# A fused layer's forward and backward pass: feed-forward spread over the table chain, gates by chunk, turned weights in the weights' slots, state sums begun beside the last d h

## The chip, the cores and the metric

The kernel runs on one core of one Trainium2 chip. The core has a matrix engine (TensorE, PE in the profile, with PEld for its weight loads), a vector engine (VectorE, DVE), a scalar engine for functions and copies (ScalarE, ACT), GpSimd (POOL), a queue engine that only issues transfers (SyncE, SP), and 16 DMA engines. Each engine works through a queue of its own in order; the engines meet by semaphores. The metric is the time of one execution on the device in microseconds; lower is better.

## The reference

A state-space convolution, gated by a feed-forward net, with a residual, forward and backward (L = 2048 rows, D = 512, N = 128 states, F = 1792):

```python
xn = _layernorm(x)
dt = exp(log_dt);  K[d,l] = Re sum_n C[d,n] exp(dt*A[d,n]*l) dt*B[d,n]     # A, B, C complex
y  = irfft(rfft(pad(xn)) * rfft(pad(K)))[:L] + xn * Dskip                  # s: the long convolution
o  = silu(xn @ w1) @ w2;   g = silu(o)                                     # the feed-forward gate
out = x + s * g
# and, by jax.vjp with grad_out, the gradients of x, A_re, A_im, B_re, B_im, C_re, C_im, log_dt, Dskip, w1, w2
```

With G for grad_out the backward pass needs ds = G * silu(o) (into the convolution's backward) and do = G * s * silu'(o) (into the feed-forward's backward); then d h = (do @ w2^T) * silu'(h), d x = d h @ w1^T, dW2 = silu(h)^T do, dW1 = xn^T d h, and the gradients of the state parameters from dK.

## The kernel before

The 2048 rows lie as 128 partitions by 16 tiles (t), the 512 channels as 4 blocks b of 128. The code is made of Python generators; each `yield` ends a step, and the helpers `interleave`, `woven`, `paced`, `until` and `after` decide how the steps of several generators are mixed. The text's order gives each instruction its rank. When the program is built, each engine's queue is laid out from these ranks and from what is ready, so an instruction can stand ahead of one that comes earlier in the text; on the chip each queue then runs in the order that was laid out.

- Setup (L1032 to L1052): loads x, weights and parameters, layer norm to `xn`, constants, DFT matrices `TF`, `TI`, `F2`, `I2`.
- `chain()` (L1065): for each block, `gen_tables` (17 steps) builds exponential tables `E` and `Y` on VectorE and ScalarE (the sines `sn`, L420), and the convolution kernel by matmuls (`ps_k` L452, `ps_e` L463), copied to `KE` and stored in `Kd`; `gen_conv_x` (4 steps) transforms `xn`; `gen_conv_fwd` of the block before (9 steps) loads the kernel as `Kb`, transforms it, multiplies the spectra (`cplx_mul`, L324), transforms back and adds the skip (`S_b`, L524), stored in `Sd`. The chain holds the forward convolutions of blocks 0 to 2.
- A forward transform (`dft_fwd`, L277) is 32 matmuls (`ps_s` L286) into `dA`, one transposing DMA `dB<-dA` (L289), three steps later 32 matmuls (L298, L299). The inverse (`dft_inv`, L304) is 32 matmuls (L311), copies, 32 matmuls (L320).
- `gen_ffn_fwd` (L532): 8 chunks of 256 rows, each 7 steps of `ps_h` (L546, copied to `hT`, stored in `Hd` by GpSimd's queue, silu to `aT`) and 2 of `ps_o` (L561, copied to `ob`, stored in `Od`). It runs as the outer loop, with 1.4 chain steps for each of its 72 (L1070).
- `gen_gate_rows` (L569): after the feed-forward, loads `Od` into `do` and grad_out into `G` (two buffers), and makes `ds` and the first factor of `do` on ScalarE, GpSimd and VectorE, mixed with what is left of the chain (L1077). `gate_s` (L595) and `gen_gate_s` multiply `do` by s, block by block.
- `gen_conv_fwd(k, 3)` (L1091) with the transposing loads of `W2T` (L1087) and the first backward transform beside it.
- `gen_conv_bwd` (L629), one block after the other: forward transform of `ds` (in `w8b` buffers, two), product with the spectrum of `xn` and inverse to `dK`, product with that of K and inverse to `du`. Beside it `gen_ffn_da` (L850): per chunk 7 steps of `ps_da` (L879) and 2 of `ps_dx` (L890), with `W1T` loaded in its first step (L860); and `gen_out` (L609), the output rows. Weights 1, 2, 1 (L1096).
- Last, with pools opened anew (L1099): `gen_ssm_bwd` (L808), the state sums: `ssm_fold` (loads `GE`, matmuls L685, L687, copy `Gf`), `ssm_v` (L718), `ssm_products` (`Tp`, L728), `ssm_sums` (`psS`, L740, L744), `gen_ssm_grads`; beside it `gen_dw2` (`ps_w` L922, a chunk of 128 columns of F per step), then `gen_dw1` (`ps_w` L940, 28 steps of 16 matmuls), and `gen_ln_bwd`.

SP issues nearly all loads and the transposes; ScalarE's queue the stores of `Kd` and `dKd`; GpSimd's queue the other stores (`k.st`). Memory is given by pools; a pool that opens where another closed must wait for the old tiles' last readers.

## Time and profile before

| | us |
|---|---|
| runs shown (3) | 764.97, 772.21, 774.16; median 772.21 |
| the profiled execution | 774.27, span 772.5 |
| mean granted TensorE clock | 0.907 |

Where the named work stands in the profiled execution (first and last start, from the rows of the tiles):

| work | from | to |
|---|---|---|
| feed-forward: ps_h, ps_o | 14.6 | 250.2 |
| tables' matmuls ps_k | 71.2 | 271.1 |
| gates: first silu (L583), last gate product (L591) | 264.2 | 304.8 |
| last forward convolution: Kb issued, last product of do with S_b | 290.1 | 333.7 |
| d h and d x: ps_da, ps_dx | 336.3 | 529.5 |
| backward convolutions' last inverse (L320) | | 507.3 |
| state sums psS | 561.6 | 724.1 |
| dW1's matmuls (L940) | 683.2 | 764.1 |

A busy time is the time in which the engine held an instruction; matmuls overlap, so that a full TensorE shows more matmul time than it gives columns. The idle time of an engine matters only where nothing else is the bound of that stage, so the profile is read by stages. DMA shares are the mean over 16 engines and can pass 1.

### The profile page before, as it was taken

The numbers are of one execution on the slowest core, as the hardware profiler recorded it, in microseconds if no ns is written. First come the engines' busy times: TensorE is split into PE (matmuls) and PEld (weight loads), VectorE is DVE, ScalarE is ACT, GpSimd is POOL, SyncE is SP. The second block draws the span as 40 slices with busy tenths as digits, with TensorE's granted clock in tenths as the row PEclk, the third lists the DMA queues.
The fourth block names the chain that finished last, engine by engine and source line by source line (L and its number), as shares of the span: only waits on it lengthen the run. The fifth ranks groups of instructions, "written<-read, shape, count | busy, mean of one in ns | idle before, by whom it ended". The sixth has DMA issues, their size and how long they took to land. (4 is left out here: it accounts for less than half of the span.)

```text
span 772.5 us, 13734 instructions
## 1 busy us (share of the span) xinstructions
PE 599.6 (78%) x5388; PEld 428.5 (55%) x5388; DVE 551.2 (71%) x1118; ACT 501.8 (65%) x700; POOL 87.3 (11%) x167
## 2 busy tenths in 40 slices
PE   3378878988979533578888798994489977899795
PEld 2244554754755333356566475672466654678675
DVE  6987997795775997489787696961163876998500
ACT  6877766877779575459878597750286677864121
POOL 2120100000000144000000000000000003130230
PEclk9699988999999785799999899997599998999998
DMA  9877866588667949999969768234899999776482
GB/s 270 305 165 240 233 212 167 231 232 239 240 189 206 348 159 212 292 307 321 269 199 259 193 183 223 65 116 108 209 221 223 270 302 255 194 140 129 79 172 71
DMA packets 218097, 163.18 MB, mean 211 GB/s; under 512 B 143024, under 2 KB 196272, under 8 KB 214192
## 3 DMA queue, kind: packets, MB, share of 16 engines
q1 hardware_dynamic: 205056, 139.75, 67.7%
q0 software_dynamic: 6224, 18.10, 6.8%
q10 hardware_dynamic: 6752, 4.46, 1.9%
q8 instruction: 42, 0.69, 0.4%
q14 instruction: 23, 0.19, 0.1%
HBM read 65.40 MB, written 62.26 MB: 165 GB/s over the span
## 5 line engine op out<-in xcount | busy, mean ns | idle before, releaser
L42 ACT CAST dA<-ps_s 128x1024 bf16<-128x1024 f32 x96 | 93.8, 1031 | 40.4 <-PE ps_s L299 24.6
L728 DVE TENSOR_TENSOR Tp<-Vb,Eb 128x1344 bf16<-128x1344 bf16 x64 | 52.6, 854 | 22.7 <-ACT Vb L42 13.7
L546 PE MATMUL ps_h<-XT,W 128*128 128x256 bf16 x448 | 61.0, 283 | 8.2 <-ACT hT L42 6.8
L42 ACT CAST dB<-ps_i 128x1024 bf16<-128x1024 f32 x48 | 46.9, 1018 | 27.5 <-PE ps_i L311 21.3
L561 PE MATMUL ps_o<-W,aT 128*128 128x512 bf16 x224 | 59.7, 408 | 5.1 <-ACT aT L554 3.9
L311 PE MATMUL ps_i<-I,sp_in 128*128 128x256 bf16 x384 | 53.0, 287 | 12.4 <-DVE sp_in L334 11.1
L298 PE MATMUL ps_s<-dB,F 128*128 128x512 bf16 x96 | 41.5, 432 | 25.6 <-DMA dB<-dA 23.1
L879 PE MATMUL ps_da<-doT,W2T 128*128 128x256 bf16 x448 | 56.5, 275 | 2.9 <-DVE dhT L881 2.9
L940 PE MATMUL ps_w<-dh_tok,xn 128*128 128x256 bf16 x448 | 53.0, 273 | 1.4 <-DMA dh_tok<-DHd 1.0
L546 PEld LDWEIGHTS <-W 128*128 128x128 bf16 x448 | 44.5, 102 | 17.2 <-issue 7.8
L890 PE MATMUL ps_dx<-W1T,dhT 128*128 128x512 bf16 x224 | 53.8, 380 | 0.0
L922 PE MATMUL ps_w<-do,a_tok 128*128 128x512 bf16 x224 | 53.0, 385 | 0.0
L311 PEld LDWEIGHTS <-sp_in 128*128 128x128 bf16 x384 | 37.5, 102 | 25.9 <-DVE sp_in L334 14.5
L286 PEld LDWEIGHTS <-TF 128*128 128x128 bf16 x384 | 27.4, 106 | 43.3 <-DMA Kb<-Kd 17.3
L879 PEld LDWEIGHTS <-W2T 128*128 128x128 bf16 x448 | 43.8, 99 | 12.4 <-issue 4.9
L42 ACT CAST Vb<-ps_v 128x672 bf16<-128x672 f32 x64 | 42.6, 723 | 9.4 <-PE ps_v L718 7.9
L42 ACT CAST o<-ps_w 128x256 bf16<-128x256 f32 (+1 forms) x42 | 18.6, 442 | 43.6 <-PE ps_w L940 31.7
L940 PEld LDWEIGHTS <-xn 128*128 128x128 bf16 x448 | 42.8, 98 | 7.1 <-issue 2.6
L881 DVE SCALAR_TENSOR_TENSOR dhT<-dhT,ps_da 128x512 bf16<-128x512 bf16 x56 | 37.2, 681 | 12.9 <-PE ps_da L879 12.6
L299 PE MATMUL ps_s<-dB,F 128*128 128x512 bf16 x96 | 41.4, 431 | 0.0
L561 PEld LDWEIGHTS <-aT 128*128 128x128 bf16 x224 | 22.0, 104 | 29.6 <-issue 7.4
L452 PEld LDWEIGHTS <-Y 128*128 128x128 bf16 x512 | 26.3, 106 | 21.7 <-DVE Y L439 11.2
(226 smaller groups left out, 1365.5 us busy)
## 6 DMA issues: line engine op xcount, KB each, us to landing
Yd<-Y SPq DMA_DIRECT2D x8, 1024.0 KB, 5.4
sp_in<-Ud SPq DMA_DIRECT2D x8, 1024.0 KB, 7.0
...
```

The costliest lines, as they stand in the source:

```text
L42: return self.nc.scalar.copy(out=out, in_=in_)
L298: nc.tensor.matmul(out=ps[:, 4 * u:4 * u + 4], lhsT=F2[:, m0], rhs=B[:, 0, g0:g0 + 4, :], start=True, stop=False)
L299: nc.tensor.matmul(out=ps[:, 4 * u:4 * u + 4], lhsT=F2[:, m1], rhs=B[:, 1, g0:g0 + 4, :], start=False, stop=True)
L311: nc.tensor.matmul(out=ps[:, g], lhsT=Y[:, c, g0 + g, :], rhs=k.I2[:, c].rearrange("p c m -> p (c m)"), start=(c == 0), stop=(c == 1))
L546: nc.tensor.matmul(out=ps[:, j], lhsT=k.W1[:, dk, ft * P:ft * P + P], rhs=XTv[:, :, dk, :], start=(dk == 0), stop=(dk == DK - 1))
L561: nc.tensor.matmul(out=ps[:], lhsT=aT[:, ft, t * P:t * P + P], rhs=k.W2[:, ft, :], start=(ft == 0), stop=(ft == FT - 1))
L728: k.nc.vector.tensor_tensor(out=Tp[:, c, :, r ^ c].rearrange("p e (q w) a -> p q w e a", w=2), in0=Vb[:, :, c].rearrange("p q w (e a) -> p ...
L879: nc.tensor.matmul(out=ps[:, j], lhsT=W2T[:, dk, ft * P:ft * P + P], rhs=dTv[:, :, dk, :], start=(dk == 0), stop=(dk == DK - 1))
L881: nc.vector.scalar_tensor_tensor(out=dh[:, i0:i0 + 2, :], in0=dh[:, i0:i0 + 2, :], scalar=1.0, in1=ps[:], op0=ALU.add, op1=ALU.mult)
L890: nc.tensor.matmul(out=ps[:], lhsT=dhs[ft // 8][:, ft % 8, t * P:t * P + P], rhs=k.W1T[:, ft, :], start=(ft == 0), stop=(ft == FT - 1))
L922: nc.tensor.matmul(out=ps[:], lhsT=at[:, t, :], rhs=k.do[:, t, :], start=(t == 0), stop=(t == k.T - 1))
L940: nc.tensor.matmul(out=ps[:], lhsT=k.xn[:, t, dk * P:dk * P + P], rhs=dh[:, t].rearrange("p j n -> p (j n)"), start=(t == 0), stop=(t == k ...
```

## The change

It does seven things.

1. The chain becomes the outer loop and the feed-forward is drawn at 0.45 steps for each chain step. What is left of the feed-forward runs beside the last forward convolution and the gates, with weights 3, 1, 1.
2. The gates go by chunk of two tiles, as the feed-forward gives them: `rows_done` says how far it is; the last chunks are read from `ob` in place instead of loaded from `Od`. grad_out is loaded at once (`Gr`). The product with s of blocks 0 to 2 is part of the gate, that of block 3 follows the convolution.
3. `do` takes the memory of the two `Y` tables, `ds` and the gates that of the table pool.
4. `W2T` is loaded into `W1`'s slot, in the last feed-forward chunk, and `W1T` into `W2`'s, by four transposes in the first d h steps.
5. `dft_fwd` runs its first half by component and turns each component by a DMA of its own.
6. `gen_conv_bwd` weaves the forward transform of the next block with the rest of this one, on six buffers; its spectra are loaded a step earlier, and so are the loads of `gen_out`. It is the outer loop (1.7 steps of d h and output rows for each).
7. The state sums begin when the backward convolutions are issued, half a step for each step of d h that is left; then they go on beside dW2 and dW1.

Smaller things: the last `Sd` store moves to ScalarE's queue, and `gen_ssm_grads` copies its turned rows back into `outb`.

```diff
+BR, SR = 1.7, 0.5
...
-def dft_fwd(k, w8, U, ev, tag="w8"):
+def dft_fwd(k, w8, U, ev):
-    A = w8.tile([P, 2, 16, P], BF16, name="dA", tag=tag)
+    A = w8.tile([P, 2, 16, P], BF16, name="dA", tag="w8")
     Av = A[:].rearrange("p c g (t e) -> p c g t e", e=8)
-    for h in range(2):
-        for c in range(2):
+    B = w8.tile([P, 2, 16, P], BF16, name="dB", tag="w8")
+    for c in range(2):
+        for h in range(2):
             ps = pc.tile([P, 8, P], F32, name="ps_s1", tag="pc")
             for j in range(8):
                 nc.tensor.matmul(out=ps[:, j], lhsT=k.TF[:, 8 * h + j, c, :], rhs=U(8 * h + j), start=True, stop=True)
             ev(Av[:, c, :, 8 * h:8 * h + 8, :], ps[:].rearrange("p t (g e) -> p g t e", e=8))
-    B = w8.tile([P, 2, 16, P], BF16, name="dB", tag=tag)
-    nc.sync.dma_start_transpose(B[:].rearrange("p c g k -> p (c g) k"), A[:].rearrange("p c g k -> p (c g k)"))
+        nc.sync.dma_start_transpose(B[:, c], A[:, c].rearrange("p g k -> p (g k)"))
     for _ in range(LAG):
         yield
...
-    nc.sync.dma_start(k.Sd[b], S[:].rearrange("p t d -> p (t d)"))
+    (nc.scalar if b == 3 else nc.sync).dma_start(k.Sd[b], S[:].rearrange("p t d -> p (t d)"))
...
-        ob = fp.tile([P, 2, D], BF16, name="ob", tag="ob", bufs=1)
+        if c == T // 2 - 1:
+            k.W2T = k.wt.tile([P, DK, k.F], BF16, name="W2T", tag="wa")
+        ob = fp.tile([P, 2, D], BF16, name="ob", tag="ob", bufs=2)
         for t in range(2):
             ps = k.pf.tile([P, D], F32, name="ps_o", tag="pf")
             for ft in range(FT):
                 nc.tensor.matmul(out=ps[:], lhsT=aT[:, ft, t * P:t * P + P], rhs=k.W2[:, ft, :],
                                  start=(ft == 0), stop=(ft == FT - 1))
             k.evf(ob[:, t], ps[:])
+            if c == T // 2 - 1:
+                for i in (2 * t, 2 * t + 1):
+                    nc.sync.dma_start_transpose(k.W2T[:, :, 448 * i:448 * i + 448], k.ins["B_w2"][448 * i:448 * i + 448, :])
             yield
         k.st(k.Od[:, 2 * c:2 * c + 2, :], ob[:])
-
-
-
-def gen_gate_rows(k, gp):
+        k.rows_done = c + 1
+        if k.late:
+            k.ob[c] = ob
+
...
+def gen_gate_rows(k, gp, lag):
 
     nc = k.nc
     TT = nc.vector.tensor_tensor
...
-    for t in range(0, 16, 8):
-        nc.sync.dma_start(k.do[:, t:t + 8, :], k.Od[:, t:t + 8, :])
-    for t0 in range(0, 16, 4):
-        G = gp.tile([P, 4, k.D], BF16, name="G", tag="G", bufs=2)
-        nc.sync.dma_start(G[:], k.g_v[:, t0:t0 + 4, :])
-        for t in range(t0, t0 + 4, 2):
-            ts = slice(t, t + 2)
-            Gt = G[:, t - t0:t - t0 + 2, :]
-            o = k.do[:, ts, :]
-            g = gp.tile([P, 2, k.D], BF16, name="g", tag="g", bufs=3)
...
-            TT(out=k.ds[:, ts, :], in0=Gt, in1=g[:], op=ALU.mult)
...
+    last = k.T // 2
+    Gr = gp.tile([P, k.T, k.D], BF16, name="Gr")
+    for t in range(0, k.T, 4):
+        nc.sync.dma_start(Gr[:, t:t + 4, :], k.g_v[:, t:t + 4, :])
+    for c in range(last):
+        while k.rows_done <= c or (c not in k.ob and k.rows_done < min(c + 1 + lag, last)):
             yield
-
-
-def gate_s(k, b, t0, n, S):
-
-    do = k.do[:, t0:t0 + n, b * P:b * P + P]
-    k.nc.vector.tensor_tensor(out=do, in0=do, in1=S, op=ALU.mult)
-
-
-def gen_gate_s(k, b, gp):
-    for t in (0, 8):
-        S = gp.tile([P, 8, P], BF16, name="S", tag="go_x", bufs=2)
-        k.nc.sync.dma_start(S[:].rearrange("p t d -> p (t d)"), k.Sd[b][:, P * t:P * t + 1024])
-        gate_s(k, b, t, 8, S[:])
-    yield
+        ts = slice(2 * c, 2 * c + 2)
+        o = k.do[:, ts, :]
+        src = o
+        if c in k.ob:
+            src = k.ob.pop(c)[:]
+        else:
+            nc.sync.dma_start(o, k.Od[:, ts, :])
+        G = Gr[:, ts, :]
+        S = gp.tile([P, 3, 2, P], BF16, name="S", tag="S", bufs=2)
+        nc.sync.dma_start(S[:].rearrange("p b t d -> p b (t d)"), k.Sd[0:3, :, 256 * c:256 * c + 256].rearrange("b p n -> p b n"))
+        if src is o:
+            yield
+        g = gp.tile([P, 2, k.D], BF16, name="g", tag="g", bufs=3)
+        nc.scalar.activation(out=g[:], in_=src, func=ACT.Silu)
+        nc.scalar.activation(out=o, in_=src, func=ACT.Tanh, scale=0.5)
+        TT(out=k.ds[:, ts, :], in0=G, in1=g[:], op=ALU.mult)
+
...
+        TT(out=o, in0=o, in1=G, op=ALU.mult)
+        o3 = o[:, :, 0:3 * P].rearrange("p t (b d) -> p b t d", b=3)
+        TT(out=o3, in0=o3, in1=S[:], op=ALU.mult)
+        yield
...
 def gen_out(k, pool):
@@ -612,52 +620,65 @@
     TT = nc.vector.tensor_tensor
     for c in range(k.T // 2):
         ts = slice(2 * c, 2 * c + 2)
+        S = pool.tile([P, 4, 2, P], BF16, name="go_s", tag="go_s", bufs=2)
+        nc.sync.dma_start(S[:].rearrange("p b t d -> p b (t d)"), k.Sd[:, :, 256 * c:256 * c + 256].rearrange("b p n -> p b n"))
         g = pool.tile([P, 2, k.D], BF16, name="go_g", tag="go_g", bufs=1)
         nc.sync.dma_start(g[:], k.Od[:, ts, :])
+        x = pool.tile([P, 2, k.D], BF16, name="go_x", tag="go_x", bufs=1)
+        nc.sync.dma_start(x[:], k.x_v[:, ts, :])
+        rows = lambda ap: ap.rearrange("p t (b d) -> p b t d", b=4)
+        yield
         nc.scalar.activation(out=g[:], in_=g[:], func=ACT.Silu)
-        S = pool.tile([P, 4, 2, P], BF16, name="go_s", tag="go_s", bufs=1)
-        nc.sync.dma_start(S[:].rearrange("p b t d -> p b (t d)"), k.Sd[:, :, 256 * c:256 * c + 256].rearrange("b p n -> p b n"))
-        x = pool.tile([P, 2, k.D], BF16, name="go_x", tag="go_x", bufs=2)
-        nc.sync.dma_start(x[:], k.x_v[:, ts, :])
-        gv = g[:].rearrange("p t (b d) -> p b t d", b=4)
-        TT(out=gv, in0=gv, in1=S[:], op=ALU.mult)
+        TT(out=rows(g[:]), in0=rows(g[:]), in1=S[:], op=ALU.mult)
         TT(out=x[:], in0=x[:], in1=g[:], op=ALU.add)
         k.st(k.o0_v[:, ts, :], x[:])
         yield
 
...
-def gen_conv_bwd(k, b):
+def gen_conv_bwd(k):
...
-    DS, A2 = yield from dft_fwd(k, dft, lambda t: k.ds[:, t, bs], k.evc, "w8b")
-    yield
-    U = spectrum_in(k, dft, b, "U")
-    KX = spectrum_in(k, dft, b, "K")
...
+    DS = {}
+
+    def forward(b):
+        bs = slice(b * P, b * P + P)
+        DS[b] = yield from dft_fwd(k, dft, lambda t: k.ds[:, t, bs], k.evc)
+        yield
+
+    def rest(b):
+        bs = slice(b * P, b * P + P)
+        U = spectrum_in(k, dft, b, "U")
+        KX = spectrum_in(k, dft, b, "K")
+        yield
+        A, A2 = DS.pop(b)
+        dK = dft.tile([P, 4, 16, 32], BF16, name="dK", tag="t4")
+        cplx_mul(k, dft, A, U, conj=True)
+
...
+        yield from dft_inv(k, A2, U, k.evc, consume_dk)
+        nc.scalar.dma_start(k.dKd[b].rearrange("a i (r s) x -> (i r) a (s x)", s=2), dK[:].rearrange("p a t q -> p a (t q)"))
+        yield
+        cplx_mul(k, dft, A, KX, conj=True)
...
+        yield from dft_inv(k, A2, KX, k.evc, consume_dx)
+        nc.sync.dma_start(k.dUd[b], du[:].rearrange("p t d -> p (t d)"))
+        yield
+    yield from forward(0)
+    for b in range(4):
+        yield from woven([forward(b + 1), rest(b)] if b < 3 else [rest(b)], [1, 1])
...
-    go = sb.tile([P, 6, P], BF16, name="go", tag="go")
     pt = k.pt.tile([P, 6, P], BF16, name="pt_g", tag="pt")
     for i in range(6):
         nc.tensor.transpose(out=pt[:, i], in_=outb[:, i], identity=k.ident[:])
-    nc.scalar.copy(out=go[:], in_=pt[:])
+    nc.scalar.copy(out=outb[:], in_=pt[:])
     for i in range(6):
-        k.st(k.outs[2 + i][bs, :], go[:, i])
+        k.st(k.outs[2 + i][bs, :], outb[:, i])
...
-        if c == 0:
-            nc.sync.dma_start_transpose(k.W1T[:], k.ins["B_w1"])
...
+            if c == 0 and f < 4:
+                nc.sync.dma_start_transpose(k.W1T[:, :, P * f:P * f + P], k.ins["B_w1"][P * f:P * f + P, :])
...
-    k.p1 = pool("p1", side="right", es=es_x)
+    es_d = ctx.enter_context(ExitStack())
+    wt = k.wt = pool("wt", es=es_d)
+    k.W1 = wt.tile([P, k.DK, F], BF16, name="W1", tag="wa")
+    k.W2 = wt.tile([P, k.FT, D], BF16, name="W2", tag="wb")
+    k.p1 = pool("p1", es=es_f)
     k.fp = pool("fp", es=es_f)
-    k.W1 = k.fp.tile([P, k.DK, F], BF16, name="W1")
-    k.W2 = k.fp.tile([P, k.FT, D], BF16, name="W2")
...
+    YD = pool("yd", side="right").tile([P, 8192], BF16, name="YD")
+    k.Y = [YD[:, 4096 * h:4096 * h + 4096].rearrange("p (c q j a) -> p c q j a", c=2, q=16, a=4) for h in range(2)]
+    k.do = YD[:].rearrange("p (t d) -> p t d", d=D)
...
-    k.Y = [k.tbl.tile([P, 2, 16, 32, 4], BF16, name="Y%d" % h) for h in range(2)]
...
-    ch = chain()
-    paced(gen_ffn_fwd(k), ch, 1.4)
+    k.rows_done, k.late, k.ob = 0, False, {}
+    ffn = gen_ffn_fwd(k)
+    paced(chain(), ffn, 0.45)
+    es_t.close()
+    k.late = True
+    k.ds = pool("ds", side="right", es=es_x).tile([P, 16, D], BF16, name="ds")
+    es_g = es_x.enter_context(ExitStack())
+    gates = gen_gate_rows(k, pool("gate", side="right", es=es_g), 1)
+
+    interleave([gen_conv_fwd(k, 3), ffn, gates], [1, 3, 1])
+    for t in (slice(0, 8), slice(8, 16)):
+        last = k.do[:, t, 3 * P:4 * P]
+        nc.vector.tensor_tensor(out=last, in0=last, in1=k.S_b[:, t], op=ALU.mult)
     es_f.close()
-    k.do = pool("fd").tile([P, 16, D], BF16, name="do")
-    es_g = ctx.enter_context(ExitStack())
-    k.ds = pool("ds", es=es_g).tile([P, 16, k.D], BF16, name="ds")
-    es_h = ctx.enter_context(ExitStack())
-    gp = pool("gate", es=es_h)
-    run(woven([gen_gate_rows(k, gp), ch], [1, 4]))
-    es_h.close()
-    es_t.close()
-    k.dftb = dft_pool("dftb", es_g, {"cm2": 1, "xd": 1, "dD": 1, "w8b": 2}, k.dft)
-    da = pool("da", side="right", es=es_x)
-    k.W2T = da.tile([P, k.DK, F], BF16, name="W2T")
-    k.W1T = da.tile([P, k.FT, D], BF16, name="W1T")
-
-    def weights():
-        for q in range(4):
-            nc.sync.dma_start_transpose(k.W2T[:, :, 448 * q:448 * q + 448], B_w2[448 * q:448 * q + 448, :])
-            yield
-            yield
-    bwd = after(5, chained(gen_conv_bwd(k, b) for b in range(4)))
-    until(gen_conv_fwd(k, 3), [weights(), bwd])
-    for t in (0, 8):
-        gate_s(k, 3, t, 8, k.S_b[:, t:t + 8])
-    for b in range(3):
-        run(gen_gate_s(k, b, da))
-    interleave([bwd, gen_ffn_da(k, da), after(12, gen_out(k, da))], [1, 2, 1])
+    es_g.close()
+    base = dft_pool("dftb", es_x, {"cm2": 1, "xd": 1, "dD": 1, "w8b": 2}, k.dft, side="right")
+    turn = itertools.cycle(["w8"] * 4 + ["w8b"] * 2)
+    k.dftb = SimpleNamespace(tile=lambda shape, dt, name, tag: base.tile(shape, dt, name=name, tag=next(turn) if tag == "w8" else tag))
+    da = pool("da", es=es_d)
+    k.W1T = wt.tile([P, k.FT, D], BF16, name="W1T", tag="wb")
+    bwd = gen_conv_bwd(k)
+    out = gen_out(k, da)
+    for i in range(4):
+        next(bwd)
+    ffb = gen_ffn_da(k, da)
+    paced(bwd, woven([ffb, out], [2, 1]), BR)
     es_x.close()
-    es_g.close()
-    sb = pool("sb")
-    fw = pool("fw", side="right")
-    interleave([gen_ssm_bwd(k, sb), chained([gen_dw2(k, fw), gen_dw1(k, fw)]), after(8, gen_ln_bwd(k, fw))], [2, 1, 1])
+    sb = pool("sb", side="right")
+    ssm = gen_ssm_bwd(k, sb)
+    paced(ffb, ssm, SR)
+    run(out)
+    es_d.close()
+    fw = pool("fw")
+    interleave([ssm, chained([gen_dw2(k, fw), gen_dw1(k, fw)]), after(8, gen_ln_bwd(k, fw))], [2, 1, 1])
```

48 lines of the change are left out of this document (18 added, 30 removed).

## The prediction

> **What bounds the kernel now.** I read four views in this order: the busy table of the page, a table of stages, the order of time of TensorE and of the SP queue around the two emptiest stages, and the waits of a few tiles.
>
> ```profile
> span 772.5 us, 13734 instructions
> PE 599.6 (78%) x5388; PEld 428.5 (55%) x5388; DVE 551.2 (71%) x1118; ACT 501.8 (65%) x700; POOL 87.3 (11%) x167
> ```
>
> No engine is full, so no single one is the bound; the stages have different ones. The stage table (start:end, length, then busy us of PE, PEld, DVE, ACT, POOL, granted clock, DMA share, GB/s):
>
> ```profile
> 50.00:250.00 200.00, 171.31 (x1574) 114.28 (x1572) 157.82 (x323) 157.58 (x238) 16.73 (x25) 0.95 0.71 217
> 250.00:336.00 86.00, 44.09 (x338) 29.65 (x337) 67.07 (x95) 47.86 (x63) 21.70 (x17) 0.74 0.90 254
> 336.00:511.00 175.00, 151.88 (x1270) 108.96 (x1269) 141.99 (x201) 132.89 (x136) 6.47 (x12) 0.95 0.75 215
> 511.00:530.00 19.00, 18.86 (x118) 11.29 (x116) 9.75 (x15) 4.57 (x6) 0.00 (x0) 1.00 0.47 141
> 530.00:555.00 25.00, 3.77 (x29) 2.97 (x30) 3.61 (x4) 3.08 (x3) 0.00 (x0) 0.56 0.75 178
> 555.00:735.00 180.00, 158.83 (x1688) 122.11 (x1685) 129.62 (x343) 116.19 (x192) 24.89 (x46) 0.95 0.84 198
> 735.00:772.50 37.50, 27.88 (x250) 24.17 (x250) 0.28 (x1) 5.95 (x16) 7.14 (x12) 0.95 0.58 125
> ```
>
> Two stages leave TensorE idle: 250 to 336 (44.09 us busy of 86, clock 0.74) and 530 to 555 (3.77 of 25, clock 0.56). The full stages run TensorE at 86 to 88% (171.31/200, 151.88/175, 158.83/180) with VectorE at 72 to 81%. Their causes, in order of time:
>
> ```profile
> 262.84 16.98 SPq L577 DMA_DIRECT2D G<-in_grad_out_dram  x2
> 286.05 0.33 SPq L527 DMA_DIRECT2D Sd<-S_b  x1
> 290.12 0.38 SPq L511 DMA_DIRECT2D Kb<-Kd  x1
> 290.60 11.79 SPq L1087 DMA_TRANSPOSE W2T<-in_B_w_dram  x4
> 303.59 5.85 SPq L289 DMA_TRANSPOSE dB<-dA  x1
> ...
> 275.77 0.99 PE L463 MATMUL ps_e<-Xr,SEL 128*128 128x224 bf16 x12
> 295.63 1.89 PE L286 MATMUL ps_s<-Kb,TF 128*128 128x128 bf16 x16 [17.08 <-DMA Kb<-Kd]
> 333.70 0.68 DVE L598 TENSOR_TENSOR do<-do,S_b 128x1024 bf16<-128x1024 bf16 x1
> 336.31 0.92 PE L879 MATMUL ps_da<-doT,W2T 128*128 128x256 bf16 x7
> ...
> 523.65 6.21 PE L890 MATMUL ps_dx<-W1T,dhT 128*128 128x512 bf16 x28
> 530.98 1.15 SPq L347 DMA_TRANSPOSE par_Ar<-in_A_A_re_dram  x1
> 538.68 2.66 SPq L669 DMA_DIRECT2D GE<-dKd  x4
> 544.50 0.61 PE L685 MATMUL G<-GE,zero 128*128 128x512 bf16 x1 [14.65 <-DMA GE<-dKd]
> ```
>
> First stage: the feed-forward is used up by 251 us (its last rows are quoted below), so nothing covers the last convolution. Its kernel Kb waits on SP behind a gate load with two buffers, its transposes behind W2T. The d h needs S_b, so its first matmul comes at 336.31. Second: the last d x ends at 530, only then are the state sums' inputs loaded, and their first matmul comes at 544.50.
>
> **The change part by part.**
>
> *Feed-forward over the chain.* Before, 72 feed-forward steps drew 1.4 chain steps each; the chain has 111 steps (21 + 3x30, counted in the generators). Now each chain step draws 0.45, which is 50 steps, and 22 (2.4 chunks of 8) are left for the last convolution and the gates. What the chain gains is seen on VectorE:
>
> ```profile
> 50.00:264.00 214.00, 178.15 (x1622) 117.99 (x1620) 171.20 (x349) 163.92 (x246) 17.29 (x26) 0.94 0.73 224
> 264.00:286.00 22.00, 11.71 (x124) 9.00 (x122) 20.27 (x25) 18.13 (x30) 11.06 (x8) 0.81 0.62 229
>   ACT sn L420: 33.6, 13
> ```
>
> VectorE idles 214 - 171.2 = 42.8 us before the gates begin at 264; 33.6 of it waits for the sines on ScalarE, which stand behind evacuations. The chain ends at 286 (the Sd row) and has about half of the 20.27 us after 264, so its VectorE work from 50 is 171 + 10 = 181 us. If none of the idle goes it ends at 50 + 181 + 43 = 274, if all the sine waits go at 240. With a third less feed-forward on ScalarE I take half: 253.
>
> *Gates by chunk.* The gate's arithmetic stays:
>
> ```profile
> L589 DVE TENSOR_TENSOR do<-do,g 128x1024 bf16<-128x1024 bf16 x8 | 8.6, 1081 | 1.9 <-POOL g L588 0.9 <-POOL do L587 0.9
> L585 DVE TENSOR_TENSOR ds<-G,g 128x1024 bf16<-128x1024 bf16 x8 | 7.0, 894 | 2.9 <-DMA G<-in_grad_out_dram 2.5 <-PE ps_i L311 0.5
> L591 DVE TENSOR_TENSOR do<-do,G 128x1024 bf16<-128x1024 bf16 x8 | 6.9, 863 | 0.1
> L590 DVE TENSOR_SCALAR do<-do 128x1024 bf16<-128x1024 bf16 x8 | 4.0, 506 | 0.0
> L598 DVE TENSOR_TENSOR do<-do,S 128x1024 bf16<-128x1024 bf16 x6 | 4.1, 687 | 0.7 <-DMA S<-Sd 0.6
> L587 POOL TENSOR_SCALAR do<-do 128x1024 bf16<-128x1024 bf16 x8 | 11.7, 1469 | 14.5 <-ACT do L584 14.5
> L588 POOL TENSOR_SCALAR g<-g 128x1024 bf16<-128x1024 bf16 x8 | 9.6, 1208 | 13.4 <-DVE ds L585 13.4
> ```
>
> That is 8.6 + 7.0 + 6.9 + 4.0 = 26.5 us of VectorE, and the three first blocks of S are multiplied in 8 pieces of 768 columns for 6 of 1024, the same 6144 columns, 4.1 us. All of grad_out is loaded at once, so SP no longer stands 17 us behind G. SP issues 8 loads of S for 6, and 5 of Od for 2 (three chunks are read where they lie), some 0.38 us each as the Kb row: 2 us, covered. New waits: do now lies in the Y tables and ds in the table pool, so no gate starts before the tables end; Kb is issued ahead of these loads, and only gates and their loads queue behind. The gates' GpSimd work now shares its queue with the feed-forward's stores, which wait for ScalarE. I price that at nothing to one store's mean wait, 135.9/16 = 8.5 us, from this row, and take nothing, as VectorE has the convolution meanwhile:
>
> ```profile
> POOL Hd L555 <- ACT hT L42: 135.9, 16, 16.9
> ```
>
> *Start of the d h.* The last ps_e ended at 276.8, 9 us ahead of the chain's end; so 244 now. Kb took 295.63 - 290.12 = 5.5 us from issue to first matmul; for copying the sums out and storing Kd I allow as much again. From there to the last S_b product took 333.70 - 295.63 = 38 us, of which some 3 were W2T ahead of the transpose. So 244 + 11 + 35 = 290, plus 3 to the first d h matmul: 293. But VectorE has 158 + 67 = 225 us of work between 50 and 336; by 293 it would run at 93%, against 79% in 50 to 250. At 88% it is 50 + 256 = 306. I take 306 for 336, a gain of 30. Ends: 293, and 330 (DMA rival below).
>
> *Turned weights.* W2T waits for the last ps_h, W1T for the last ps_o. W1T's one transpose becomes four; dB's 12 become 24 halves, the first issued when half of dA is there. Issue time goes with size:
>
> ```profile
> L289 SPq DMA_TRANSPOSE dB<-dA x12: 4749/5367/6992, 53.8 to 469.2; - x12
> L707 SPq DMA_TRANSPOSE YT<-Yd x32: 1237/1497/3758, 541.4 to 696.1; - x32
> ```
>
> A YT is a quarter of a dB and takes 1497 against 5367/4 = 1342 ns, so a half costs at most some 0.1 to 0.2 us more: 12 x 0.3 = 4 us of SP, hidden under waits; the earlier start saves at most one half's 2.7 us per transform on the chain. Taken as nothing either way. The last Sd store goes from SP to ScalarE's queue, under 1 us there; the go tile's removal costs nothing.
>
> *Convolution backward.* Forward b+1 now runs beside the rest of b with six buffers (before, two for A and B, so one block after the other). It ends sooner relative to the d h: 32 of its steps draw 54, of which 38 of the d h's 72. The work is the same.
>
> *State sums beside the last d h.* 34 d h steps are left; 17 state steps go with them. The hole of 25 us goes, as 72 - 38 = 34 steps of matmuls cover the 14 us from SP's first load to the sums' first matmul; what is late next is that fold itself. I leave 5 us (none to 14). The matmuls of dW1 then stand alone: 28 steps for some 16 before.
>
> ```profile
> 750.25 14.13 PE L940 MATMUL ps_w<-dh_tok,xn 128*128 128x256 bf16 x128 [1.04 <-DMA dh_tok<-DHd]
> ```
>
> 128 in 14.13 us, with the wait of 1.04 some 0.118 each: 448 are 53 us, and 772.5 - 764.4 = 8 us of stores end the kernel: a tail of 61 for 37.5. What stands before it, in TensorE busy time from 336 on, is 151.88 + 18.86 + 3.77 + 158.83 + 27.88 - 50 = 311 us. At the 87% of the full stages that takes 357 (at 84%: 370; at 92%: 338).
>
> *Sum.* 306 + 357 + 5 + 61 = 729 us of span. The profiled execution took 774.27 for a span of 772.5, so 2 more: 731. The median of the runs shown is 772.21, lower by 0.3%, so I say 729.
>
> *A rule against it.* Gate products run beside GpSimd: the L589 row has 1081 ns, with single ones of 1.52 us beside 0.68 us for the same shape. By rows the excess over 0.68 (0.41 for L590) is 3.2 + 1.7 + 1.5 + 0.8 = 7 us, and it is in the sum. The Trainium skill, page "SBUF — State Buffer", section "SBUF: two separate sides", says that GpSimd and VectorE share one pair of ports and that whichever starts first holds it for its whole instruction. The trace agrees for single products. By that rule the sum could be up to the whole GpSimd time worse than free running, for which the third rival has the number.
>
> **The rivals.**
>
> 1. *The program's order holds, and it gets slower.* If the 22 late steps ran only after the chain, at the old pace of at most 250/72 = 3.5 us, and the chain gained nothing, the last of it would come at 286 + 77 = 363, W2T (11.79 us to issue) at 375, and the end at 375 + 423 + 2 = 800. It decides from a first d h matmul at 788 - 425 = 363 on. Against it:
>
> ```profile
> 87.50 3.18 PE L561 MATMUL ps_o<-W,aT 128*128 128x512 bf16 x13
> 95.03 0.38 PE L561 MATMUL ps_o<-W,aT 128*128 128x512 bf16 x1
> 99.88 1.02 PE L463 MATMUL ps_e<-Xr,SEL 128*128 128x512 bf16 x4 [0.17 <-ACT Xr L42]
> 249.77 0.81 PE L561 MATMUL ps_o<-W,aT 128*128 128x512 bf16 x3
> ```
>
> The third chunk's output (the third set of 28) is done at 95, ahead of the first block's last step at 99.88, though the program puts 15 steps, 1.7 chunks, before that. So work is pulled forward when the queues are built, as it will be now. Chance 0.08.
>
> 2. *DMA holds the gates' stage.* Its share is 0.90 of 86 us, 77 us of work. If that must pass after 253, the d h starts at 330 and the time is 753. For: W2T, loads and halves of dB crowd there. Against: part of those loads came from 250 to 264. Chance 0.12.
>
> 3. *GpSimd blocks VectorE throughout the gates* (the rule above, to its end): 11.7 + 9.6 = 21.3 us instead of 7, on VectorE as that stage's bound: +14, 743. Chance 0.07.
>
> 4. *The second half gains nothing*: the filled hole is paid back in the longer tail, 306 + 436.5 + 2 = 744. For: VectorE's share of the sums is fixed. Against: the hole's 25 us hold almost no work of any engine. Chance 0.13.
>
> **How the numbers follow.** My forecast, 729 with 704 to 748 as its own range (293 + 338 + 61 = 692 and 317 + 370 + 14 + 61 = 762 are its far ends, unlikely together), has 0.50; a mixture of rivals 2 to 4 in which both halves gain nothing, about 770, has 0.10. About 2% can be told from no change here, that is 757 and 788. Faster: 0.50 + 0.13 + 0.07 + 0.08 of rival 2 = 0.78. Slower: rival 1, 0.08. The same: 0.14. The range from 697 to 760 leaves out rival 1 and the mixture.
>
> **What would show it.** Right: no TensorE idle of 17 us before Kb; the last ps_e near 244; first ps_da between 293 and 330; ps_h still running beside the gates; the first G matmul before the last ps_dx, and no hole there; ps_w of dW1 alone for over 50 us at the end. Wrong: a first ps_da after 336, a TensorE wait of over 10 us for GE, DMA shares of 1 in the gates' stage with VectorE under 85%, or ps_h standing wholly behind the chain.

## The result, and the profile after

The changed kernel takes 742.0 us (median of 4 runs, 737.61 to 744.94) beside 770.92 for the kernel before on the same chip: a ratio of 0.963 (95% interval 0.955 to 0.971), 3.7% faster. Forecast were 729 us and a range of 697 to 760. The profiled execution has a span of 743.2 us; at 744.94 us it is the longest of its four, so its stages are to be read with some 3 us of allowance. One execution of the plain loads below took 1485.14 us and is left out of their time and ratio.

The page's first lines, and the stage table (start:end, length, busy us of PE, PEld, DVE, ACT, POOL, granted clock, DMA share, GB/s), cut where the changed kernel's stages lie:

```profile
span 743.2 us, 13798 instructions
PE 600.7 (81%) x5388; PEld 427.2 (57%) x5388; DVE 546.6 (74%) x1120; ACT 500.9 (67%) x700; POOL 92.0 (12%) x167
```

```profile
50.00:250.00 200.00, 161.55 (x1569) 110.85 (x1568) 173.13 (x354) 156.48 (x235) 16.12 (x22) 0.95 0.80 239
250.00:320.00 70.00, 47.39 (x331) 31.25 (x331) 47.35 (x62) 49.27 (x65) 24.73 (x20) 0.76 0.95 229
320.00:488.00 168.00, 147.68 (x1209) 103.48 (x1208) 136.62 (x197) 123.87 (x129) 7.33 (x12) 0.96 0.80 220
488.00:545.00 57.00, 50.63 (x485) 38.53 (x486) 38.87 (x52) 33.91 (x43) 0.00 (x0) 0.91 0.92 209
545.00:680.00 135.00, 119.64 (x1220) 85.35 (x1219) 102.55 (x292) 92.26 (x151) 22.50 (x42) 0.95 0.87 214
680.00:743.20 63.20, 50.82 (x455) 43.12 (x452) 6.93 (x26) 11.62 (x30) 9.52 (x15) 0.96 0.55 118
```

TensorE's busy time is about the same (600.7 us for 599.6): what went is idle time. The hole of 25 us ahead of the state sums is gone, and the stage of the gates is shorter but as thin as it was: 47.39 of 70 us on TensorE (68%; before, 51%). The rows of the tiles give where the work lies (count, shortest/median/longest ns, first and last start):

```profile
L465 PE MATMUL ps_e<-Xr,SEL x96: 219/259/635, 94.3 to 257.7; 128*128 128x224 bf16 x32, 128*128 128x128 bf16 x32, 128*128 128x512 bf16 x16, 128*128 128x160 bf16 x16
L565 PE MATMUL ps_o<-W,aT x224: 376/379/635, 40.0 to 293.6; 128*128 128x512 bf16 x112
L899 PE MATMUL ps_da<-doT,W2T x448: 269/273/418, 320.3 to 543.3; 128*128 128x256 bf16 x150
L706 PE MATMUL G<-GE,zero x8: 229/304/631, 488.2 to 596.7; 128*128 128x512 bf16 x4, 128*128 128x160 bf16 x4
L960 PE MATMUL ps_w<-dh_tok,xn x448: 269/273/283, 679.7 to 734.8; 128*128 128x256 bf16 x150
```

| | before | forecast | after |
|---|---|---|---|
| last ps_e | 276.5 | 244 | 257.7 |
| Kb's first matmul | 295.6 | 255 | 269.0 |
| last product of do with S_b | 333.7 | 290 | 321.0 |
| first ps_da | 336.3 | 306 | 320.3 |
| from there to the end of the span | 436.2 | 423 | 422.9 |

So the second half came out as forecast, and the whole miss, 14 us, lies ahead of the first d h: 16 us were gained there for 30. The order of time of SP, PE, ScalarE and VectorE in that stage:

```profile
243.01 8.42 SPq L596 DMA_DIRECT2D YD<-Od  x2
263.87 0.37 SPq L513 DMA_DIRECT2D Kb<-Kd  x1
272.99 9.85 SPq L291 DMA_TRANSPOSE dB<-dA  x2
...
259.15 4.05 PE L565 MATMUL ps_o<-W,aT 128*128 128x512 bf16 x18
263.91 1.95 PE L322 MATMUL ps_i<-dB,TI 128*128 128x128 bf16 x32
269.03 1.06 PE L289 MATMUL ps_s<-Kb,TF 128*128 128x128 bf16 x16
282.53 1.01 PE L300 MATMUL ps_s<-dB,F 128*128 128x512 bf16 x2 [3.64 <-DMA dB<-dA]
320.29 1.65 PE L899 MATMUL ps_da<-doT,W2T 128*128 128x256 bf16 x7 [2.02 <-ACT doT L44]
...
259.42 2.84 ACTq L489 DMA_DIRECT2D Kd<-KE  x4
262.30 1.01 ACT L44 CAST dB<-ps_i 128x1024 bf16<-128x1024 f32 x1 [2.00 <-issue]
...
265.00 1.23 DVE L526 TENSOR_TENSOR S_b<-ps_i,xd 128x1024 bf16<-128x1024 f32 x1 [12.22 <-PE ps_i L322]
301.78 1.52 DVE L609 TENSOR_TENSOR YD<-YD,g 128x1024 bf16<-128x1024 bf16 x1
321.00 0.68 DVE L1105 TENSOR_TENSOR YD<-YD,S_b 128x1024 bf16<-128x1024 bf16 x1
```

VectorE stands idle for 12.2 us until block 2's inverse (L322) comes. On PE, 18 late feed-forward matmuls stand ahead of it, but the last copy (dB) that it needs ends on ScalarE only at 263.3, behind the stores of Kd that hold that queue for 2.84 us. Then come Kb's transform, two transposes that hold SP 9.85 us, and the rest of the convolution among gate products, to 321. From Kb's first matmul to the last product it is 52 us where 35 were forecast.

### The profile page after: what moved, and what is told of

It is laid out like the page before. It is cut to its first block, busy times and chain, and to the rows that moved or that the text cites. A ratio compares the mean times of both kernels' runs of the same rounds, so it can differ in the third digit from the quotient of the medians.

```text
span 743.2 us, 13798 instructions
## 1 busy us (share of the span) xinstructions
PE 600.7 (81%) x5388; PEld 427.2 (57%) x5388; DVE 546.6 (74%) x1120; ACT 500.9 (67%) x700; POOL 92.0 (12%) x167
## 4 chain that ended last, share of the span: by engine, by line
issue 28%; DVE 23%; DMA 16%; PE 16%; ACT 10%; POOL 4%; SPq 2%; ACTq 0%; POOLq 0%; DVEq 0%
PE ps_dx L910 3%; ACT dA L44 3%; DMA dB<-dA 3%; PE ps_o L565 3%; PE ps_da L899 2%; DVE sp_in L335 2%; DVE W L449 2%; DMA YT<-Yd 1%; DMA Pd<-pd_s 1%; PE ps_i L313 1%; DVE YD L441 1%; DMA Kb<-Kd 1%; DVE m L440 1%; DMA Ud<-dA 1%; ACT sn L422 1%
## 5 line engine op out<-in xcount | busy, mean ns | idle before, releaser
L899 PE MATMUL ps_da<-doT,W2T 128*128 128x256 bf16 x448 | 63.7, 283 | 6.8 <-DVE dhT L901 2.6
L548 PE MATMUL ps_h<-XT,W 128*128 128x256 bf16 x448 | 63.9, 291 | 6.3 <-ACT hT L44 4.5
L313 PE MATMUL ps_i<-I,sp_in 128*128 128x256 bf16 x384 | 54.2, 285 | 13.7 <-ACT dD L664 5.3
L910 PE MATMUL ps_dx<-W1T,dhT 128*128 128x512 bf16 x224 | 55.3, 392 | 0.0
L313 PEld LDWEIGHTS <-sp_in 128*128 128x128 bf16 x384 | 37.1, 102 | 30.6 <-DVE sp_in L336 13.7
L942 PE MATMUL ps_w<-YD,a_tok 128*128 128x512 bf16 x224 | 53.6, 386 | 0.0
L960 PE MATMUL ps_w<-dh_tok,xn 128*128 128x256 bf16 x448 | 50.5, 273 | 2.5 <-DMA dh_tok<-DHd 2.4
L300 PE MATMUL ps_s<-dB,F 128*128 128x512 bf16 x96 | 36.9, 390 | 14.1 <-DMA dB<-dA 9.0
L301 PE MATMUL ps_s<-dB,F 128*128 128x512 bf16 x96 | 36.0, 382 | 4.2 <-DMA dB<-dA 4.2
L739 PE MATMUL ps_v<-Gb,YT 128*128 128x168 bf16 x256 | 29.8, 250 | 10.6 <-ACT Vb L44 8.9
```

The costliest lines, as they stand in the source:

```text
L300: nc.tensor.matmul(out=ps[:, 4 * u:4 * u + 4], lhsT=F2[:, m0], rhs=B[:, 0, g0:g0 + 4, :], start=True, stop=False)
L301: nc.tensor.matmul(out=ps[:, 4 * u:4 * u + 4], lhsT=F2[:, m1], rhs=B[:, 1, g0:g0 + 4, :], start=False, stop=True)
L313: nc.tensor.matmul(out=ps[:, g], lhsT=Y[:, c, g0 + g, :], rhs=k.I2[:, c].rearrange("p c m -> p (c m)"), start=(c == 0), stop=(c == 1))
L548: nc.tensor.matmul(out=ps[:, j], lhsT=k.W1[:, dk, ft * P:ft * P + P], rhs=XTv[:, :, dk, :], start=(dk == 0), stop=(dk == DK - 1))
L899: nc.tensor.matmul(out=ps[:, j], lhsT=W2T[:, dk, ft * P:ft * P + P], rhs=dTv[:, :, dk, :], start=(dk == 0), stop=(dk == DK - 1))
L910: nc.tensor.matmul(out=ps[:], lhsT=dhs[ft // 8][:, ft % 8, t * P:t * P + P], rhs=k.W1T[:, ft, :], start=(ft == 0), stop=(ft == FT - 1))
```

## The experiments

Two things are asked: what holds the first d h at 320 and not 306 (transfers, GpSimd, the memory shared with the tables, late feed-forward or late gates), and whether the second half was right for the reason given. Each ratio is to the kernel before, on the chip of its own batch. The changed kernel itself stands at 0.963 (0.955 to 0.971), so a ratio within about 0.8% of that is not told from it; those of one transpose, of 0.65 steps and of grad_out by chunks (0.9703 to 0.9705) lie just within it.

**Plain loads of the turned weights.** W2T and W1T are filled by plain loads of w1 and w2, so that d h, d x and dW1 come from other values.

```diff
-nc.sync.dma_start_transpose(k.W2T[:, :, 448 * i:448 * i + 448], k.ins["B_w2"][448 * i:448 * i + 448, :])
+nc.sync.dma_start(k.W2T[:, i, :], k.ins["B_w1"][P * i:P * i + P, :])
...
-nc.sync.dma_start_transpose(k.W1T[:, :, P * f:P * f + P], k.ins["B_w1"][P * f:P * f + P, :])
+nc.sync.dma_start(k.W1T[:, :, P * f:P * f + P], k.ins["B_w2"].rearrange("(k p) d -> p k d", p=P)[:, :, P * f:P * f + P])
```

> The changed kernel, but W2T and W1T are filled by plain loads of the same 1.8 MB each (of the untransposed weights, so d h and d x use other values). It takes their eight transposing DMAs out of the gates' stage. Changed kernel: 742 us, ratio 0.963, first ps_da at 320.3. DMA-crowding theory (the transposes of the weights hold SP and the 16 DMA engines while the last convolution's own transposes and the gates' loads of S wait): first ps_da 306 to 312, time 728 to 735, ratio about 0.947. GpSimd-port theory, shared-memory theory and queue-order theory: first ps_da within 3 us of 320, ratio within 0.005 of 0.963.

Measured: 746.16 us (median of three), 0.9644 (0.9605 to 0.9683); the first ps_da at 318.9. So the weights' transposes do not set the end of the stage; the bytes of their loads were still moved.

**GpSimd's gate products on VectorE** (L607 and L608 by `nc.vector`).

> The changed kernel with the gates' two GpSimd products (L607, L608) on VectorE. Port theory (GpSimd's 21 us of products block VectorE and add a hop between engines to each gate): the gate products at 1.5 us fall to 0.68, VectorE gains 7 us of blocking and takes 16 x 0.41 = 6.6 us of new work, the hop of some 2 us a gate goes, so first ps_da 312 to 316 and ratio 0.953 to 0.958. DMA-crowding theory: no change, 320 and 0.963, or 0.97 if VectorE is the bound there.

Measured: 744.52 us, 0.9635 (0.9596 to 0.9675); the first ps_da at 323.3. The order of time on VectorE, then the stage's row:

```profile
298.83 0.42 DVE L607 TENSOR_SCALAR YD<-YD 128x1024 bf16<-128x1024 bf16 x1
300.11 0.68 DVE L609 TENSOR_TENSOR YD<-YD,g 128x1024 bf16<-128x1024 bf16 x1
```

```profile
250.00:320.00 70.00, 42.75 (x331) 27.88 (x330) 44.98 (x81) 51.84 (x67) 2.85 (x4) 0.84 0.98 236
```

With 19 more instructions VectorE is busy 2.4 us less (44.98 for 47.35): all eight products L609 take 0.68 us, where in the changed kernel, beside GpSimd, they take 0.68 to 1.52. The Trainium skill, page "SBUF — State Buffer", section "SBUF: two separate sides", has the two engines share one pair of ports, held for a whole instruction; these durations agree. The time does not move, so these products, on either engine, are not what sets it.

**Gates on rows of their own.** The loads of Od and the gate's intermediates go to four buffers `w` instead of into do, which lies in the Y tables.

```diff
+w = gp.tile([P, 2, k.D], BF16, name="w", tag="w", bufs=4)
...
-nc.sync.dma_start(o, k.Od[:, ts, :])
+nc.sync.dma_start(w[:], k.Od[:, ts, :])
...
```

> The changed kernel with the gate's loads and intermediate products in four buffers of their own (w) and only the last product written to do, which shares memory with the Y tables. Shared-memory theory (the first gate waits for the last store of Y, 8.4 us, and stands on ScalarE's queue ahead of the copies of the last table, and on SP the loads of Od stand ahead of grad_out and Kb): ScalarE's wait of 3.3 us at 251 goes, Kb is issued 3 to 8 us before 263.9, first ps_da 312 to 317, ratio 0.952 to 0.959. DMA-crowding theory: Kb may come earlier but the first ps_da stays within 3 us of 320, ratio 0.960 to 0.965.

Measured: 764.73 us, 0.9877 (0.9814 to 0.994). ScalarE's wait of 3.27 us for the last store of Y, at 251.08 in the changed kernel, is gone, and Kb is issued at 261.0 in place of 263.9. But seven other kernels here with the shared rows and the same chain issue Kb at 261.4 to 265.0, so a gain at Kb is not shown. And the loads of Od now come at 267 to 298 (at 238 to 251 in the changed kernel): the first behind all of grad_out's on SP, two more behind the transposes of dB. ScalarE waits up to 5.6 us for them, and the first ps_da comes at 330.3. The run therefore does not say what the shared memory costs.

**One transpose for both components**, as before the change.

```diff
-        nc.sync.dma_start_transpose(B[:, c], A[:, c].rearrange("p g k -> p (g k)"))
+    nc.sync.dma_start_transpose(B[:].rearrange("p c g k -> p (c g) k"), A[:].rearrange("p c g k -> p (c g k)"))
```

> The changed kernel with the forward transform's first half and its transposing DMA as before: one transpose of 1 MB after both components instead of two of 0.5 MB. If halves cost too much on SP (24 of median 3.46 us against 12 of 5.37 is 19 us more): 2 to 6 us faster, ratio 0.955 to 0.960. If their earlier start is worth it: up to one half's 3 us for each of some eight transforms on the chain, 5 to 15 us slower, ratio 0.97 to 0.98. If hidden: 0.963 within 0.004.

Measured: 750.2 us, 0.9703 (0.9676 to 0.973). The ratio alone is not told from the changed kernel's. But the last ps_e comes at 263.2 for 257.7, later than in any kernel here that keeps the halves (251.3 to 259.8), TensorE's matmuls L300 wait 34.5 us for dB in place of 9.7, and the first ps_da comes at 325.8 for 320.3:

```profile
50.00:250.00 200.00, 158.28 (x1469) 106.15 (x1467) 165.59 (x344) 151.31 (x227) 14.35 (x17) 0.93 0.76 226
```

VectorE does 7.5 us less in the 200 us of the chain. So the halves, which the prediction priced at nothing, carry some 5 us in these two executions, and the chain is where.

**How much feed-forward the chain draws:** 0.65 of a step, then 0.55, for 0.45.

```diff
-    paced(chain(), ffn, 0.45)
+    paced(chain(), ffn, 0.65)
```

> Each of the chain's 111 steps draws 0.65 of a feed-forward step in place of 0.45, so all 72 run within the chain and none of the 22 is left for the last convolution. Theory A (the 22 late steps are what stretches the stage from Kb to the first ps_da to 51 us after Kb's first matmul at 269: their matmuls and evacuations stand ahead of the last transform and their chunks are what the gates wait for): with them gone the stage falls to some 40 us; the chain, with more work on ScalarE and TensorE beside it, ends later than after's 257.7 by up to 22 x 2.1 = 46 us of TensorE work less its idle time, say 10 us; first ps_da 310 to 325, time 733 to 747. Theory B (the stage is the chain of the last convolution and the gates' arithmetic, the feed-forward steps fill gaps in it): the stage stays 51 and only moves later by the chain's 10 us and more: first ps_da from 330 on, time 752 or more, and TensorE is emptier in it than the 47 of 70 us of after.

> Each chain step draws 0.55 of a feed-forward step: 61 in the chain, 11 left for the last convolution and the gates. Between after and the kernel with 0.65. Theory A (late steps stretch the stage): 735 to 744, first ps_da 313 to 321. Theory B (they fill gaps): 745 to 750, half of what the kernel with 0.65 loses.

Measured: with 0.65, 751.29 us, 0.9705 (0.9635 to 0.9775); with 0.55, 742.98 us, 0.9613 (0.9541 to 0.9686), not told from the changed kernel, although its first ps_da comes at 326.7; its profiled execution, 748.89 us, was the longest of four. That time lies in theory A's range and that ps_da outside it, so 0.55 decides nothing. With 0.65 the stage is emptier, by the stage table, and SP issues Kb behind both turned weights, by its order of time:

```profile
250.00:320.00 70.00, 31.30 (x192) 20.57 (x190) 42.49 (x57) 39.63 (x46) 25.89 (x17) 0.62 0.82 230
```

```profile
251.35 8.80 SPq L570 DMA_TRANSPOSE W2T<-in_B_w_dram  x2
260.31 1.41 SPq L596 DMA_DIRECT2D YD<-Od  x3
261.81 9.45 SPq L891 DMA_TRANSPOSE W1T<-in_B_w_dram  x4
271.31 0.58 SPq L586 DMA_DIRECT2D Gr<-in_grad_out_dram  x1
272.00 0.37 SPq L513 DMA_DIRECT2D Kb<-Kd  x1
```

From Kb's issue to the first ps_da it is 56.6 us (272.0 to 328.6), against 56.4 (263.9 to 320.3) with 22 late steps: the stage is no shorter without them, as theory B has it, although here W1T's transposes too lie ahead of Kb. And the last ps_e does not come later with more feed-forward in the chain, as both theories expected: it comes at 253.8 with 0.55 and at 251.3 with 0.65, where the kernels with 0.45 and two halves have 253.9 to 259.8.

**The state sums behind the d h.** The rest of the d h runs out before the first step of the sums is written down.

```diff
+    run(ffb)
     ssm = gen_ssm_bwd(k, sb)
-    paced(ffb, ssm, SR)
```

> The rest of the d h steps runs out before the first step of the state sums is built, as before the change; the conv's backward stays woven. Theory of the prediction (the hole before the sums was nearly free of work, so filling it gains; the tail only moves matmuls): a TensorE wait of 10 us or more for GE comes back and a stretch of some 25 us with TensorE under a third, the tail shrinks from 63 us to about 40, and of the 13 us that the second half gained (423 for 436 from the first ps_da to the end) most goes: 750 to 757. Rival 4 of the prediction (the filled hole is paid back in the tail): 742 within 3 us, first ps_da to the end 423 to 426.

Measured: 752.55 us, 0.9735 (0.9672 to 0.9799); the first ps_da at 318.9, from there to the end 432.2. The first sums' matmul stands at 499.0, still ahead of the last ps_dx (523.5), since the queues are laid out when the program is built and steps are pulled forward: no hole and no wait for GE. But TensorE is thinner, by the stage table:

```profile
488.00:515.00 27.00, 21.15 (x133) 14.23 (x132) 12.43 (x19) 12.10 (x10) 0.00 (x0) 0.87 0.83 212
515.00:545.00 30.00, 25.11 (x228) 18.07 (x227) 15.38 (x19) 15.84 (x22) 0.00 (x0) 0.94 0.65 152
...
680.00:751.10 71.10, 56.62 (x579) 49.23 (x576) 25.44 (x83) 15.20 (x36) 12.01 (x20) 0.95 0.52 105
```

From 488 to 545 it is busy 46.26 us for 50.63, with VectorE at 27.81 for 38.87: the sums' products, which are VectorE's, come later, still take 25.44 us of it in the last stage (6.93), and leave TensorE idle there for 14.5 us (12.4). So in this execution the time is lost to thinner stages and not to a hole; the wait that was expected back did not come. Rival 4 falls all the same: the second half takes 436.2 us in the kernel before and at most 432.2 in any kernel of this document.

**The convolution's backward, one block after the other.**

```diff
-    yield from forward(0)
     for b in range(4):
-        yield from woven([forward(b + 1), rest(b)] if b < 3 else [rest(b)], [1, 1])
+        yield from forward(b)
+        yield from rest(b)
```

> The convolution's backward runs one block after the other again (first transform of a block, then its rest) in the order of its steps, with the six buffers kept. Theory (the weave of blocks changes the order of the same work; the 13 us of the second half are the filled hole): 742 to 746, first ps_da to the end 423 to 427. Rival (the weave is what gains, by giving each transposed transform time to land): 750 to 756, with TensorE waits for dB of several us in each of three blocks between the first ps_da and the first G matmul.

Measured: 753.25 us, 0.9743 (0.9683 to 0.9802); the first ps_da at 318.1, from there 431.4. The time is the rival's, its mechanism is not: no matmul waits for dB longer than 1.6 us, and TensorE does the same from 320 to 488 (147.18 us for 147.68). But the backward convolutions end later (last inverse L322 at 487.9 instead of 467.1), the sums begin at 505.9 instead of 488.2, and the d h's end is covered less (TensorE busy 46.42 us from 488 to 545 for 50.63).

**Gates without their arithmetic.**

```diff
-        nc.gpsimd.tensor_scalar(out=o, in0=o, scalar1=-0.5, scalar2=0.5, op0=ALU.mult, op1=ALU.add)
...
-        TT(out=o3, in0=o3, in1=S[:], op=ALU.mult)
```

> Leaves out the gates' arithmetic behind silu, tanh and the first product (the two GpSimd operations and the four VectorE products of each of eight chunks, L607 to L613, 31 us of VectorE); the loads, the state product and everything after stay, so d h is computed from other values. Theory D (the 52 us from Kb's first matmul to the last state product, forecast 35, are the last convolution's steps standing among late gates on VectorE): 52 falls to 35 to 40, first ps_da 303 to 309, time 725 to 732. Rival E (they are the convolution's own chain through the transposed transfers, which the crowded DMA stretches): the stretch stays within 4 us of 52, first ps_da 316 to 321, time 738 to 743.

Measured: 742.55 us, 0.9611 (0.9567 to 0.9654). The order of time on VectorE, ScalarE and PE:

```profile
309.07 0.69 DVE L1098 TENSOR_TENSOR YD<-YD,S_b 128x1024 bf16<-128x1024 bf16 x1
...
312.43 1.06 ACT L624 ACTIVATE go_g<-go_g 128x1024 bf16<-128x1024 bf16 x1 [4.68 <-DMA go_g<-Od]
313.40 1.91 ACT L44 CAST dA<-ps_s 128x1024 bf16<-128x1024 f32 x2
316.40 1.02 ACT L44 COPY doT<-pt_t 128x1024 bf16<-128x1024 bf16 x1
...
319.48 1.03 PE L300 MATMUL ps_s<-dB,F 128*128 128x512 bf16 x2 [4.02 <-DMA dB<-dA]
320.30 3.97 PE L892 MATMUL ps_da<-doT,W2T 128*128 128x256 bf16 x24
```

Theory D is right about the stretch and wrong about the time. From Kb (270.2) to the last product it is 38.9 us, as D expected: late gates on VectorE make 13 of the 17 us by which the forecast missed. But the first d h comes at 320.3 all the same. ScalarE's queue has the first output row ahead of the copy doT and waits for its load, and PE's has the first backward transform ahead of the d h and waits for its transposes. The gates' work is covered by the next wait.

**grad_out by chunks**, each with its gate's loads, in three buffers, in place of `Gr` at once.

> grad_out is loaded by chunks of two row groups, each with its gate's other loads (three buffers), in place of four large loads ahead of the gates. Theory E (three of the four large loads follow Kb at 264 to 269 and crowd the DMA while dB is transposed, 9.85 us for two halves with the DMA share above 1): the two transposes issue in 6 to 7 us, the second transform starts 3 us earlier, first ps_da 314 to 318, time 736 to 740. Theory D (late gates on VectorE): no gain from the transposes, and gates whose rows now come later: first ps_da 320 to 326, time 742 to 748.

Measured: 750.15 us, 0.9704 (0.9677 to 0.9731). The order of time on SP:

```profile
269.84 2.06 SPq L291 DMA_TRANSPOSE dB<-dA  x1
271.94 1.41 SPq L598 DMA_DIRECT2D S<-Sd  x2
273.45 5.10 SPq L291 DMA_TRANSPOSE dB<-dA  x1
```

As theory E has it, the halves take 7.2 us on SP for 9.85, and the first ps_da comes at 316.7. But from there to the end it is 431.4 us: TensorE is busy 141.86 us of 320 to 488 for 147.68. What was gained ahead of the d h was lost behind it; why is not shown.

**Kd's last stores on SP** (`(nc.sync if b == 3 else nc.scalar)` at L489).

> The last block's four stores of the kernel sums Kd are issued on SP, where Kb follows them, in place of ScalarE, where a copy that block 2's inverse waits for stands behind their 2.84 us. If that issue time is on the path: block 2's inverse and the first gates' VectorE work come 2 to 3 us earlier than 265, Kb 1 us earlier than 263.9, first ps_da 317 to 320, time 739 to 742. If the late feed-forward matmuls ahead of that inverse hold it (18 of them, 259.15 to 263.20): no change, 742 within 3.

Measured: 751.99 us, 0.9722 (0.9677 to 0.9766). Block 2's inverse comes at 263.4 for 263.9, although the matmuls L313 that feed it start 2.1 us later in this execution (259.87 for 257.73): with the stores gone from ScalarE, some 2 us were to be had. But Kb, issued on SP behind these stores and block 2's Sd, comes at 268.3, and all four loads of grad_out follow it; VectorE waits 7.7 us for the first of them, and the first ps_da is at 323.3.

**The output rows beside dW1**, the attempt at a faster kernel.

```diff
...
-    paced(bwd, woven([ffb, out], [2, 1]), BR)
+    paced(bwd, ffb, BR * 2 / 3)
...
-    run(out)
...
-    interleave([ssm, chained([gen_dw2(k, fw), gen_dw1(k, fw)]), after(8, gen_ln_bwd(k, fw))], [2, 1, 1])
+    interleave([ssm, chained([gen_dw2(k, fw), gen_dw1(k, fw)]), after(8, gen_ln_bwd(k, fw)), after(20, gen_out(k, fw))], [2, 1, 1, 1])
```

> The eight output steps (loads of S, of the feed-forward's rows and of x; silu, a product, a sum and a store) leave the stretch behind the gates and run beside dW1, where VectorE is busy 7 of 63 us and ScalarE 12. Theory F (with the gates' arithmetic gone the state product ended 12 us earlier and the first d h still came at 320.3: what stands there is ScalarE waiting for the first output load and the transfers of a stretch whose DMA share is above 1 from 275 to 350, so work taken off the DMA and out of ScalarE's order there is gain): first ps_da 315 to 319, DMA share from 310 to 350 down from 1.1 to under 1, and with 12 us of ScalarE and VectorE less from 320 to 488 the TensorE share there rises from 88% to 90 or 92; time 730 to 738. Rival: the output steps filled gaps only, and beside dW1 they are free too, since TensorE sets that stage: 740 to 744. If their loads or stores hold dW1 or end after it: 745 or more.

Measured: 742.63 us, 0.963 (0.9589 to 0.9671), the changed kernel's own ratio. The stage table, then the row of dW1's tile:

```profile
320.00:488.00 168.00, 155.23 (x1302) 109.74 (x1302) 133.90 (x189) 124.53 (x132) 2.04 (x4) 0.97 0.72 190
680.00:705.00 25.00, 19.45 (x164) 16.35 (x162) 3.94 (x6) 5.32 (x12) 5.99 (x10) 0.93 1.06 266
```

```profile
L960 PE MATMUL ps_w<-dh_tok,xn x448: 269/273/418, 665.7 to 728.4; 128*128 128x256 bf16 x150
```

TensorE fills 92% from 320 to 488 for 88%, as theory F had it, and dW1 begins 14 us earlier (665.7 for 679.7). But the first ps_da stays at 320.8, and dW1 takes 62.7 us for 55.1, with the DMA share at 1.06: its loads now share the DMA with those of the output rows. TensorE's waits for them rise only from 2.4 to 5.5 us, so this accounts for a part of the 7.6 us. About half of the 14 us is given back in the tail of this one profiled execution, which was also the shortest of its six runs; the medians show no gain.

## Why the prediction was right, and where it was wrong

**Direction and second half: right; its parts less so.** From the first d h the terms 357, 5 and 61 make 423; measured 422.9 (359.4 to dW1 and 63.5 behind it). The hole is gone and the tail is about as long as worked out from the 0.118 us of a dW1 matmul. That 423 was hit to a tenth is luck: in eight kernels here whose second half is written as in the changed one it took 417.4 to 431.4. The prediction gave the gain to the hole alone and priced the weave of the backward blocks at "the same work". Undoing either raises the median by 1%, just beyond what can be told, and the second half of the profiled execution by 9 us (432.2 and 431.4); since the upper end of those eight reaches as far, the 9 us alone do not single out these edits. What does is the order: without the weave the sums begin 187.8 us after the first ps_da, in the changed kernel 167.9, in those eight 158.9 to 173.6. So the weave counts, and the likely reason is that it ends the backward convolutions earlier and lets the sums begin.

**The chain: mis-sized, for a wrong reason.** Forecast was a last ps_e at 244, by half of 42.8 us of VectorE idle time, since a third less feed-forward on ScalarE would free the sines. It came at 257.7; from 50 to 250 idle fell only from 42.2 to 26.9 us, and

```profile
  ACT sn L422: 22.8, 13
```

shows 11 of 33.6 us gone from the sines' waits. The reason given falls with the two runs that put more feed-forward into the chain and did not end it later: with 0.65 the sines are waited for even less. What did help are the halves of dB: with one transpose for both, the waits are back at 33.3 us. From 50 to 250 (us, times, longest), the kernel with one transpose, then the one with 0.65:

```profile
DVE E L429 <- ACT sn L422: 30.0, 11, 7.9
DVE H L429 <- ACT sn L422: 3.3, 1, 3.3
...
DVE E L429 <- ACT sn L422: 15.4, 11, 4.9
```

The halves were priced at nothing and bring 5.5 of the 19 us, although each holds SP longer than was allowed: 3.46 us in the median, where half of 5.37 us and at most 0.2 more were allowed. Where the other 13 us come from was not tried alone.

**Kb: right.** 11 us were allowed from the last ps_e to Kb's first matmul; it took 11.3. The order on SP was another than said, though: the five loads of Od and the first of grad_out stand ahead of Kb, the last two of Od holding SP for 8.42 us, but they were issued by 251.9, before Kb could be.

**From Kb to S_b: the step that failed.** 35 us were carried over from the kernel before, where most of the gates were done by then; measured 52. Moved gates run among the convolution's products (13 us, by the run without their arithmetic), and the two halves held SP 9.85 us where one transpose of the whole had held it 5.85.

**VectorE as the bound: wrong.** The forecast of 306 was VectorE at 88% from 50 on; up to 320 it is at 82% (220.5 of 270 us; 225 us of work were worked out), at 68% from 250 to 320 (47.35 of 70), and with 20 us of its work left out the d h begins at the same time. Six kernels that took a different load away (weights' transposes, GpSimd, the gates' products, grad_out's crowding, the output rows, late feed-forward by half) have their first ps_da at 316.7 to 326.7 and none is faster than the changed kernel beyond the intervals. The run without the gates' arithmetic shows one reason: behind the wait that was taken away stand others, in the fixed order of ScalarE's and PE's queues. That it is the same with the other five is argued, not shown. Which order would bring it near 306 stays open.

**The rivals.** Rival 1 (the program's order holds): no, ps_o ran until 293.6 and ps_da began at 320.3. Rival 2 (DMA): the weights' transposes are not it, by the plain loads; the share is 0.95 in the stage and the rest of the DMA was not taken away. Rival 3 (GpSimd): falls, 0.9635. Rival 4: falls, the second half gained 13 us.
